# Four fixed PSUM places and a new order of jobs in an attention kernel with experts behind it

## The chip, the cores and the metric

The program runs on one core of one Trainium2 chip. The metric is the device time of one execution in microseconds (us), and less is better. The engines are named as the profile names them: PE (TensorE, with its weight loads as PEld), DVE (VectorE), ACT (ScalarE), POOL (GpSimd) and SP (SyncE, which here only issues DMAs). They run side by side and wait for each other on semaphores. PSUM, where matmuls write, has eight banks of 512 floats in each of 128 partitions.

## The reference

The first half is attention for 8 batches of 8 heads, 576 positions and 64 columns a head. The second is a layer of 8 experts, of which each token goes through one.

```
q_rot, k_rot = rotate(q), rotate(k)
scores = scale * q_rot @ k_rot^T;  scores -= max(scores)
attn = exp(scores);  attn /= sum(attn) + 1e-9
x = attn @ v, as [4608 tokens, 512]
logits = x @ w_gate + modality_bias[modality_id];  e = argmax(logits)
gate = softmax(logits)[e]
out = gate * (relu(x @ w1[e]) @ w2[e])
```

## The kernel before

Two heads make a pair, and there are 32 pairs (NPAIR), four to a batch. For each pair n the kernel does these jobs, whose names are used below:

- LD and LD1 load q and k of the pair, transposed, from DRAM (two halves), and LV loads v.
- T1, T2, R, HI, LO make the rotated q and k: two products, a sum, a rounded high part HL[:, 0] (HI, on ACT) and the rest HL[:, 1] (LO). T1, T2, R and LO run on POOL except at the start. The tiles HL and SW exist twice, for even and odd pairs.
- SWH and SWL are DMAs by SP that put the two heads' halves of HL's high and low part into SW with partitions exchanged.
- S0 to S8 are score blocks of 128 queries on PE: 64-row matmuls on HL and SW, six for S0 to S7 and twelve for S8, which takes the last 64 queries of both heads. Each fills both banks of a double place `[128, 2, 512]` in PSUM. MNu is the row minimum on DVE (the scores carry a minus sign, so it is the maximum), and EXu the exponential on ACT, which also adds up the row into `sum`.
- F0 to F3, FA and FB ("fills") are PE transposes of the exponentials, 82 in all, again into a double place. A_F is the copy of its first bank to SBUF by ACT, and B_F that of its second by DVE.
- AVA and AVB multiply by v on PE (queries 0 to 255 and 256 to 575), OTA and OTB copy the result on ACT, and OUT transposes it back on PE together with the gate's weights.
- re and ri: the sums plus 1e-9 on ACT (line 406), and their reciprocal on DVE (line 409). EVA and EVB are `ev` on DVE (lines 434 to 438), which multiplies OUT's two banks by ri into X, G and XT.
- After the fourth pair of a batch, XO writes the batch's X to DRAM (SP, one DMA of 1 MB and two small ones), BIAS and the steps RK of `route` find each token's expert (POOL, DVE, ACT, one set of small PE matmuls at RK8), and the scatters SC write rows of a table (POOL).

Each job has a key, its place in one long list: the key in KEYS plus 14.438 times the pair's number (PER). The list is sorted by key and its jobs are emitted one after the other. PE, ACT, DVE, POOL and SP each keep the order of emission, so the keys alone set what stands behind what on each engine; they are not times that anything waits for. The first two and the last two pairs have keys of their own in AT (`first`, `second`, `last2`, `last`), as have the batch work and the first expert's jobs.

PSUM is divided in two. RING has three double places that scores and fills take in turn; the pool psA has two single banks for AV, OUT and the rank matmuls of RK8. A matmul that takes a place waits until its last reader has ended; `free` removes the wait for the minimum, since the exponential has waited for it already.

After the attention come blocks of 256 tokens that go through one expert each: m_l1 and m_l2 are the two matmuls, with weights split into a high and a low part on ACT and DVE (m_hi, m_lo), gathered rows transposed on DVE (m_tr) and split (m_tre). The first block's L1 is emitted among the last pair's jobs, into places of the ring.

Of the kernel before, what the change touches and what calls it, by code (L numbers as in the profile page):

```python
# [8 lines left out]
F32 = mybir.dt.float32  # L9
# [9 lines left out]
P = 128  # L19
# [22 lines left out]
    "FB": 8.21, "A_FB": 8.89, "B_FB": 9.00, "AVA": 11.22, "OTA": 13.98, "AVB": 14.84, "OTB": 18.19, "OUT": 19.01,  # L42
    "EVA": 25.51, "EVB": 20.38, "RE": 11.27, "RI": 15.89, "XO": 27.00, "T1": -32.78, "T2": -26.38,
    "R": -23.03, "LO": -15.27, "HI": -18.83, "SWH": -17.41, "SWL": -11.79, "LD": -39.33, "LV": -10.14,
}
AT = dict(
    rk=(23.0, 28.55, 31.2, 36.9, 41.45, 43.0, 44.4, 45.7, 54.6, 56.9, 57.4, 58.85, 60.2, 70.35, 73.3),
    bias=15.6,
    sc=(73.4, 87.85, 102.3, 116.7, 116.75),
    sce=(73.4, 73.45, 87.85, 87.9, 102.3),  # L50
    pl=(58.9, 70.4, 73.35, 84.85, 87.75, 99.3, 102.2, 113.7, 116.6),
    plan=(-49.7, -35.2, 6.0, 9.0),
    ix=(-41.5, -3.9, 6.1, 9.1),
    sine=-48.9,
    rows=(((0, -27.5, None), (1, -13.05, None), (2, -12.4, None), (3, -2.9, (30, "av", 0)), (5, 0.45, (30, "av", 1)),
           (7, 4.75, (30, "out", 1))), ((0, 11.15, ("l1", 0)),), ((0, 16.5, None),)),
    w1=(-21.6, -21.5, -16.2, -16.1),
    w2=(-9.9, -9.8, -9.7, -9.6),
    hi=(-14.8, -14.7, -0.4, -0.3),
    lo=(-11.8, -1.6, 10.8, 10.85),  # L60
    tr=(10.2, 10.21),
    te=(10.3, 10.4),
    hi2=(10.5, 10.98, 11.1, 11.2),
    lo2=(11.5, 11.55, 11.65, 11.75),
    last=dict(F2=7.0, A_F2=7.75, B_F2=7.75, FB=7.5, A_FB=8.3, B_FB=8.3, FA=8.35, A_FA=8.8, B_FA=8.8, AVB=10.3, AVA=10.4, RE=10.2,
              RI=10.25, OTB=10.96, OTA=11.0, OUT=11.21, EVB=11.35, EVA=11.4, XO=11.9),
    last2=dict(EVA=24.55),
    l1=(11.1, 11.3, 11.4, 11.42),
    l1e=(11.3, 11.6, 11.7, 11.8),
    w1n=(11.85, 11.86, 11.87, 11.88),  # L70
    end=12.0,

    first=dict(S1=-5.9, S0=-5.86, MN1=-5.82, MN0=-5.74, EX1=-5.7, EX0=-5.66, S6=-5.58, S7=-5.54, MN6=-5.5,
        EX6=-5.42, MN7=-5.34, EX7=-5.3, S3=-5.26, S2=-5.22, MN3=-5.18, EX3=-5.14, F0=-5.1, MN2=-5.06,
        A_F0=-5.02, B_F0=-4.98, EX2=-4.94, F3=-4.9, S4=-4.86, A_F3=-4.82, B_F3=-4.78, MN4=-4.74, S5=-4.7,
        EX4=-4.66, MN5=-4.62, EX5=-4.58, S8=-4.54, MN8=-4.5, EX8=-4.46, LV=-2.9),
    second=dict(T1=-20.22, T2=-20.06, R=-19.9, HI=-19.82),
    consts=(44.4, 51.3),
    setdma=(-2.85, 8.0, 22.5, 30.1),
    sine3=-47.5,  # L80
)
PIN = "PE,Activation,DVE,Pool"
# [3 lines left out]
def tile_attention_moe(ctx: ExitStack, tc: tile.TileContext, qk, v, mod, wg, mb, w1, w2, rope, cf, ci, out):  # L86
# [45 lines left out]
    psA = att.enter_context(tc.tile_pool(name="psA", bufs=2, space=PSUM))  # L132
# [26 lines left out]
    RING = [psS.tile([P, 2, 512], F32, name=f"ps{i}") for i in range(3)]  # L159
    lastmin = [None] * 3  # L160
    turn = [0]

    def ring():
        i = turn[0] % 3
        turn[0] += 1
        seen, lastmin[i] = lastmin[i], None
        return i, RING[i], seen

# [134 lines left out]
    def scores(n, u):  # L303
        d = st[n]
        ri, ps, seen = ring()
        d["ring", u] = ri
# [3 lines left out]
        for m, (hh, wq, wk) in enumerate(L):  # L310
            for g in range(2):
                t = d["HL" if g == hh else "SW"][g * 64:g * 64 + 64]
                k0 = K1 if g else K0
                free(nc.tensor.matmul(ps[:, g, 0:288], t[:, wq, q0:q0 + P], t[:, wk, k0:k0 + 288],  # L314
                                      start=(m == 0), stop=(m == len(L) - 1)), seen)
# [4 lines left out]
    def rowmin(n, u):  # L320
        d = st[n]
        mn = sm.tile([P, 1], F32, name="mn", tag="mn", bufs=6)
        lastmin[d["ring", u]] = nc.vector.tensor_reduce(mn, d["S", u][:, :, 0:288], op=ALU.min, axis=AX.XY).ins  # L323
        d["m", u] = mn

    def expo(n, u):
# [4 lines left out]
                             bias=d.pop(("m", u)), scale=-1.0, accum_out=d["sum"][:, u:u + 1])  # L331


    def tpose(ps, g, c, src, k0):
        r = slice(g * 64, g * 64 + 64)
        free(nc.tensor.transpose(ps[0][:, g, c:c + 64], src[r, k0:k0 + P], idf[r, r]), ps[1])  # L336

    def fill(n, f):
        d = st[n]
        ps = ring()[1:]  # L340
        d[f] = ps[0]
# [19 lines left out]
    def evac(n, f, g):  # L361
        d = st[n]
        ps = d[f][:, g]
        mine, other = (d.setdefault((f, x), []) for x in (g, 1 - g))

# [19 lines left out]
    def AV(n, half):  # L385
        d = st[n]
        c0, c1 = (0, 256) if half == 0 else (256, 576)
        pa = d["pa", half] = psA.tile([P, 512], F32, name="pa", tag="pa")
        for kt in range(5):
            for hh in range(2):  # L390
                r = PH[:, 4 * hh + kt, c0:c1] if kt < 4 else PD[:, c0:c1]
                i = nc.tensor.matmul(pa[hh * 64:hh * 64 + 64, 0:c1 - c0], d["V"][:, hh, kt, :], r, start=(kt == 0), stop=(kt == 4))  # L392
                d.setdefault(("av", half), i.ins)

    def avout(n, half):
        d = st[n]
        c0, c1 = (0, 256) if half == 0 else (256, 576)
        acopy(OT[n % 2][:, c0:c1], d.pop(("pa", half))[:, 0:c1 - c0])

    bt_ = {}  # L400

    def rsum(n, part):
        d = st[n]
        if part == 0:
            d["re"] = sm.tile([P, 9], F32, name="re", tag="re")
            nc.scalar.activation(d["re"], d["sum"], AF.Identity, bias=EPS)
        else:
            d["ri"] = sm.tile([P, 9], F32, name="ri", tag="ri")
            nc.vector.reciprocal(d["ri"], d["re"])

    def outp(n):
# [5 lines left out]
        po = [psA.tile([P, 512], F32, name="pa", tag="pa") for _ in range(2)]  # L417
        for i in range(5):
            for h in range(2):
                c = (i * P, 448 if h and i == 4 else i * P)[h]  # L420
                r = slice(h * 64, h * 64 + 64)
                x = nc.tensor.matmul(po[h][:, i * 72:i * 72 + 72], oT[r, c:c + P], RW[r, hp, :], start=True, stop=True)
                d.setdefault(("out", h), x.ins)
        d["po"] = po

    def ev(n, h):
# [11 lines left out]
        nc.vector.tensor_scalar(Bt["xt"][r, :, hp, :], po[r, 288:360].rearrange("p (o c) -> p o c", o=2), ri[r, 8:9], None, op0=ALU.mult)  # L438

# [12 lines left out]
    def route(b):  # L452
# [46 lines left out]
        pm = bank("H") if b == B - 1 else psA.tile([P, 512], F32, name="pa", tag="pa")  # L499
        pr = pm[:, 0:48].rearrange("p (j e) -> p j e", e=E)  # L500
        nc.tensor.matmul(pr, UT, OH, start=True, stop=False)
        for j in range(5):
            nc.tensor.matmul(pr[:, j + 1:6, :], ON, OH[:, j:j + 1, :].to_broadcast([P, 5 - j, E]), start=False, stop=(j == 4))
# [3 lines left out]
        V_.tensor_tensor(RUN[:, b + 1, :], pr[:, 5, :], RUN[:, b, :], op=ALU.add)  # L507
        yield
# [230 lines left out]
    spare = []  # L739
# [466 lines left out]
```

## Time and profile before

| | us |
|---|---|
| three timed runs | 933.55, 936.58, 946.05 |
| their median | 936.58 |
| the profiled execution | 934.42 |
| its span, first to last instruction | 932.6 |
| PE busy in the span | 894.4 (96%) |
| DVE, ACT, POOL busy | 682.6, 623.0, 659.1 |

The attention stage takes about the first 490 us, and the experts the rest. The profile's rows carry start and duration in us, the engine, the line of the kernel, and output<-inputs by tile names with buffer numbers left out: `ps` is any place of RING, `pa` a bank of psA, `P` the exponentials, `PH` and `PD` the transposed ones, `ST` the loaded q and k or weights, `mn` a row minimum. A PE row's end is modelled, so starts are more to be trusted than durations. In a row of a stretch of the span the columns are the stretch, its length, then busy us and instructions of PE, PEld, DVE, ACT and POOL, the granted clock, the share of the DMA engines, and GB/s.

### The profile page before, as it was taken

To read this page: it belongs to the slowest core of one execution; us is meant where nothing else is said; L and a number is where in the kernel's file an instruction comes from. 1 tells how busy PE (TensorE), PEld (TensorE's weight loads), DVE (VectorE), ACT (ScalarE), POOL (GpSimd) and SP (SyncE) were. 2 spreads that over 40 slices of the span, in tenths; PEclk is the share of its full clock that TensorE was granted. 3 is DMA by queue.
4 is the path that set the end of the run, shared out by engine and by line. 5 is a ranking of instruction groups with operands and counts; after the bars stand their busy time and mean duration, and the time that the engine had idled before them with its cause. 6 is when DMAs were issued, how large, how long until landed. Compare 5 with 4: busy or idle time off the path is not lost.

```text
span 932.6 us, 24974 instructions
## 1 busy us (share of the span) xinstructions
PE 894.4 (96%) x9248; PEld 738.7 (79%) x9248; DVE 682.6 (73%) x1221; ACT 623.0 (67%) x1291; POOL 659.1 (71%) x494
## 2 busy tenths in 40 slices
PE   2999999999999999999999999999999999999996
PEld 2777777777777777777677888888888899789996
DVE  7678788877878778787886878766666666666663
ACT  3778787787877878778783655565555555455652
POOL 4988879889888988999833677566576665556410
PEclk9999999999999999999999999999999999999999
DMA  8865757678586885856752631127635112511240
GB/s 265 246 178 171 238 157 201 196 175 238 156 199 190 184 229 155 200 179 180 203 163 75 154 109 35 55 75 244 202 97 189 50 57 92 170 57 37 79 154 21
DMA packets 82301, 141.10 MB, mean 151 GB/s; under 512 B 28635, under 2 KB 52589, under 8 KB 81148
## 3 DMA queue, kind: packets, MB, share of 16 engines
q1 hardware_dynamic: 71660, 118.25, 44.9%
q0 software_dynamic: 9248, 19.46, 6.8%
q10 hardware_dynamic: 1264, 1.72, 0.6%
q8 instruction: 75, 1.23, 0.6%
q14 instruction: 54, 0.44, 0.2%
HBM read 140.33 MB, written 19.51 MB: 171 GB/s over the span
## 4 chain that ended last, share of the span: by engine, by line
PE 67%; ACT 16%; DVE 9%; issue 4%; another core or an unknown queue 1%; DMA 1%; POOL 0%; DVEq 0%; POOLq 0%; ACTq 0%
PE psH L860 22%; PE psY L883 21%; ACT P L330 13%; PE ps L314 10%; PE pa L392 9%; DVE mn L323 6%; PE ps L336 5%; ACT PH L274 2%; DMA SW<-HL 1%; DVE PH L368 1%; DMA ST<-in_qk_dram 1%; ACT HL L274 0%; ACT W2H L274 0%; DVE PD L368 0%
## 5 line engine op out<-in xcount | busy, mean ns | idle before, releaser
L330 ACT ACTIVATE P<-ps,mn 128x576 f32<-128x576 f32 x288 | 210.4, 737 | 94.1 <-DVE mn L323 94.1
L323 DVE TENSOR_REDUCE mn<-ps 128x1 f32<-128x576 f32 x288 | 204.1, 745 | 82.9 <-PE ps L314 37.3
L795 POOL DMA_INDIRECT XG<-X,iy x148 | 181.7, 1228 | 66.8 <-issue 50.2
L860 PE MATMUL psH<-HL,W1H 128*128 128x256 f32 x1152 | 202.6, 279 | 0.0
L314 PE MATMUL ps<-SW 64*128 64x288 f32 x960 | 166.4, 313 | 15.2 <-DMA SW<-HL 15.2
L860 PEld LDWEIGHTS psH<-HL,W1H 128*128 128x128 f32 x1152 | 176.8, 188 | 1.6
L314 PE MATMUL ps<-HL 64*128 64x288 f32 x960 | 165.9, 312 | 1.6 <-ACT P L330 1.5
L860 PE MATMUL psH<-HL,W1L 128*128 128x256 f32 x576 | 160.8, 279 | 0.2 <-DVE W1L L271 0.2
L314 PEld LDWEIGHTS ps<-HL 64*128 64x128 f32 x960 | 136.5, 189 | 23.5 <-issue 12.1
L314 PEld LDWEIGHTS ps<-SW 64*128 64x128 f32 x960 | 134.3, 189 | 26.2 <-DMA SW<-HL 13.5
L271 DVE TENSOR_TENSOR W1L<-ST,W1H 128x1024 fp32r<-128x1024 f32 x76 | 90.3, 1223 | 76.6 <-ACT W1H L274 68.8
L392 PE MATMUL pa<-PH,V 128*64 128x320 f32 (+1 forms) x1024 | 138.2, 412 | 0.0
L888 POOL DMA_INDIRECT out_dram<-y,ix x36 | 46.2, 1284 | 115.3 <-ACT y L886 69.7
L883 PE MATMUL psY<-W2H,SW 128*128 128x512 f32 (+1 forms) x304 | 118.8, 391 | 1.9 <-issue 1.5
L883 PE MATMUL psY<-W2L,SW 128*128 128x512 f32 (+1 forms) x304 | 119.7, 394 | 0.0
L336 PE MATMUL ps<-idf,P 64*128 64x64 f32 x2624 | 110.6, 229 | 9.5 <-ACT P L330 3.4
L336 PEld LDWEIGHTS ps<-idf,P 64*128 64x128 f32 x2624 | 93.2, 140 | 25.4 <-ACT PH L274 9.0
L291 POOL TENSOR_TENSOR HL<-ST,HL 128x1216 fp32r<-128x1216 f32 x31 | 85.9, 2772 | 33.1 <-ACT HL L274 33.1
L860 PEld LDWEIGHTS psH<-HL,W1L 128*128 128x128 f32 x576 | 108.3, 188 | 0.4 <-DVE W1L L271 0.4
L392 PEld LDWEIGHTS pa<-PH,V 128*64 128x64 f32 x1024 | 67.9, 136 | 48.4 <-issue 10.0
L368 DVE COPY PH<-ps 128x512 f32<-128x512 f32 (+1 forms) x160 | 96.0, 629 | 10.2 <-PE ps L336 9.3
L271 DVE TENSOR_TENSOR W2L<-ST,W2H 128x1024 fp32r<-128x1024 f32 x76 | 92.5, 1218 | 4.2 <-ACT W2H L274 3.6
(197 smaller groups left out, 1575.7 us busy)
## 6 DMA issues: line engine op xcount, KB each, us to landing
ST<-in_moe_w_dram SPq DMA_DIRECT2D x152, 512.0 KB
ST<-in_qk_dram SPq DMA_DIRECT2D x62, 608.0 KB
SW<-HL SPq DMA_DIRECT2D x124, 232.0 KB
V<-in_v_dram SPq DMA_DIRECT2D x32, 256.0 KB
X<-X SPq DMA_DIRECT2D x8, 1024.0 KB
XG<-X,iy POOLq DMA_INDIRECT x148
V<-in_v_dram SPq DMA_DIRECT2D x64, 16.0 KB
X<-XT SPq DMA_DIRECT2D x16, 64.0 KB
```

The costliest lines, as they stand in the source:

```text
L271: nc.vector.tensor_tensor(o, a, b, op=ALU.subtract)
L291: e.tensor_tensor(d["HL"][:, 1, c], a, d["HL"][:, 0, c].bitcast(F32), op=ALU.subtract)
L314: free(nc.tensor.matmul(ps[:, g, 0:288], t[:, wq, q0:q0 + P], t[:, wk, k0:k0 + 288], start=(m == 0), stop=(m == len(L) - 1)), seen)
L323: lastmin[d["ring", u]] = nc.vector.tensor_reduce(mn, d["S", u][:, :, 0:288], op=ALU.min, axis=AX.XY).ins
L330: nc.scalar.activation(p.rearrange("p (a b) -> p a b", a=2), ps[:, :, 0:288], AF.Exp, bias=d.pop(("m", u)), scale=-1.0, accum_out=d["sum"] ...
L336: free(nc.tensor.transpose(ps[0][:, g, c:c + 64], src[r, k0:k0 + P], idf[r, r]), ps[1])
L368: mine.append((nc.vector.tensor_copy if g else acopy)(o, i).ins)
L392: i = nc.tensor.matmul(pa[hh * 64:hh * 64 + 64, 0:c1 - c0], d["V"][:, hh, kt, :], r, start=(kt == 0), stop=(kt == 4))
L795: inst = nc.gpsimd.indirect_dma_start(out=XG[s % 2][:, t, g, :], out_offset=None, in_=X.rearrange("n (i f) -> (n i) f", f=P)[0:rows], in_o ...
L860: l1_[s] = nc.tensor.matmul(ps[:, i, :], w[:, c, f0:f0 + P], x[:, c, :], start=(m == 0), stop=(m == 11)).ins
L883: nc.tensor.matmul(ps, hx[:, c, t * P:(t + 1) * P], x[:, c, h * w:h * w + w], start=(m == 0), stop=(m == 23))
L888: inst = nc.gpsimd.indirect_dma_start(out=out.rearrange("n (i f) -> (n i) f", f=w) if nh > 1 else out, out_offset=bass.IndirectOffsetOnAxi ...
```

## The change

There are four parts.

1. PSUM becomes one set of four double places SL. Scores, fills and OUT take both banks of a place, AVA and AVB one bank, and RK8 one bank. A table SLOTS says which place each job takes; if it isn't idle in the order of emission, another that has been idle longest is taken. A bank counts as idle once the job that reads it last has been emitted (`give`). RING and psA go.
2. KEYS is replaced, and with it the order of all jobs of a pair on PE, ACT, DVE, POOL and SP. The batch work (BIAS, RK0 to RK14, SC0 to SC4) and LD1 are in the same table now, the first expert's jobs in a table MOE, and AFTER holds what the gathers wait for.
3. The first two pairs keep an order of their own for some jobs (EDGE); the last two pairs follow KEYS.
4. The sum's guard and the reciprocal become one job RI on DVE.

```
 KEYS = {
+    "S0": 4.14, "MN0": 4.15, "EX0": 6.38, "S1": -0.75, "MN1": 0.49, "EX1": 0.96, "S2": -3.41, "MN2": -1.89, "EX2": 0.16, "S3": -6.54,
+    "MN3": -3.18, "EX3": -1.90, "S4": -7.65, "MN4": -6.15, "EX4": -4.71, "S5": -9.23, "MN5": -8.96, "EX5": -7.24, "S6": -11.86, "MN6":
+    -10.68, "EX6": -8.87, "S7": -4.99, "MN7": -2.67, "EX7": -0.77, "S8": -14.04, "MN8": -12.86, "EX8": -12.07, "F0": 7.62, "A_F0": 8.97,
+    "B_F0": 9.28, "F1": 7.75, "A_F1": 10.33, "B_F1": 9.87, "F2": -0.67, "A_F2": 0.90, "B_F2": 0.90, "F3": 1.74, "A_F3": 2.36, "B_F3":
+    1.96, "FA": 6.38, "A_FA": 7.35, "B_FA": 7.28, "FB": 1.85, "A_FB": 4.00, "B_FB": 2.71, "AVA": 11.22, "AVB": 6.10, "OTA": 15.05,
+    "OTB": 7.76, "OUT": 16.47, "EVB": 21.70, "EVA": 18.17, "RI": 9.89, "T1": -34.83, "T2": -32.09, "R": -28.61, "LO": -19.61, "HI":
+    -23.39, "SWH": -18.86, "SWL": -18.48, "LD": -40.45, "LD1": -51.82, "LV": 4.14, "XO": 23.88, "BIAS": 24.03, "RK0": 24.74, "RK1":
...
 }
+SLOTS = {
+    "S0": 3, "S1": 2, "S2": 3, "S3": 2, "S4": 3, "S5": 0, "S6": 1, "S7": 0, "S8": 3, "F0": 0, "F1": 1, "F2": 0, "F3": 1, "FA": 1, "FB":
+    0, "AVA": 1, "AVB": 2, "OUT": 2, "RK8": 5, "L1": 0,
+}
...
+MOE = dict(
...
+    l1=(12.000, 18.000, 22.400, 22.500),
...
+    end=25.0,
+)
...
-    RING = [psS.tile([P, 2, 512], F32, name=f"ps{i}") for i in range(3)]
+    SL = [psS.tile([P, 2, 512], F32, name=f"ps{i}") for i in range(4)]
+    idle = {(i, b): i * 2 + b for i in range(4) for b in range(2)}
+    def take(nm, bks):
+        own = SLOTS[nm]
...
+        if not all((own, b) in idle for b in bks):
...
+                own = min((i for i in range(4) if all((i, b) in idle for b in bks)), key=lambda i: max(idle[i, b] for b in bks))
...
+    def give(own, *bks):
+        for b in bks:
+            idle[own, b] = clock[0]
+            clock[0] += 1
...
-            nc.scalar.activation(d["re"], d["sum"], AF.Identity, bias=EPS)
+        nc.vector.tensor_scalar(d["re"], d["sum"], 1e-9, None, op0=ALU.add)
+        d["ri"] = sm.tile([P, 9], F32, name="ri", tag="ri")
+        nc.vector.reciprocal(d["ri"], d["re"])
```

In the old table XO had 27.00, SWH -17.41, SWL -11.79, EVA 25.51, EVB 20.38, LO -15.27, LV -10.14 and S8 -5.22. A job of pair n+3 has 43.314 added when it is compared with one of pair n.

More of the change, by code (lines that the diff above doesn't have):

```diff
@@ L387, in AV @@
         c0, c1 = (0, 256) if half == 0 else (256, 576)
-        pa = d["pa", half] = psA.tile([P, 512], F32, name="pa", tag="pa")
+        own, _, seen = take("AV" + "AB"[half], (half,))
+        pa = d["pa", half] = SL[own][:, half, :]
+        d["at", "av", half] = own
         for kt in range(5):
@@ L416, in outp @@
             bt_[b] = dict(x=xo.tile([P, 4, DM], F32, name="X", tag="X"), xt=xo.tile([P, 2, 4, 36], F32, name="XT", tag="XT", bufs=2))
-        po = [psA.tile([P, 512], F32, name="pa", tag="pa") for _ in range(2)]
+        own, _, seen = take("OUT", (0, 1))
+        po = [SL[own][:, h, :] for h in range(2)]
+        d["at", "out"] = own
         for i in range(5):
@@ L507, in route @@
         V_.tensor_tensor(RUN[:, b + 1, :], pr[:, 5, :], RUN[:, b, :], op=ALU.add)
+        if b < B - 1:
+            give(own, bk)
         yield
@@ L948, in tile_attention_moe @@
         K_("OUT", outp, n)
-        for w in range(2):
-            K_("R" + "EI"[w], rsum, n, w)
+        K_("RI", rsum, n)
         if n > 0:
@@ L991, in tile_attention_moe @@
[L991 to L998 removed]
+            for i, x in enumerate(steps):
+                K_(f"RK{i}", *x)
@@ L999, in tile_attention_moe @@
+    for i in range(2):
+        J(MOE["consts"][i], "consts", 0, setup2, i)
+        Z("place", i, weights2, i)
+        Z("tr", i, m_tr, 0, i)
+        Z("te", i, m_tre, 0, i)
+    g = plan0()
+    for i in range(9):
+        Z("pl", i, next, g, None)
     for s in range(3):
         for i in range(8):
-            k_, after = [x for x in A["rows"][s] if x[0] <= i][-1][1:]
-            Z(k_ + 0.01 * i, m_gather, s, i // 4, i % 4, after)
-    for i in range(2):
-        Z(min((A["hi2"], A["lo2"])[i]) - 0.01, weights2, i)
@@ L1005, in tile_attention_moe @@
[L1005 to L1018 removed]
+            Z("rows", 8 * s + i, m_gather, s, i // 4, i % 4, AFTER.get((s, i)))
```

204 lines of the change are left out of this document (89 added, 115 removed), and 13 rows, old and new, of tables (EDGE, KEYS).

## The prediction

> **What bounds the kernel now.** I read the page's busy shares first, then the stretches of the span, then the chain that ended last, and then one pair's rows in the timeline.
>
> ```profile
> span 932.6 us, 24974 instructions
> PE 894.4 (96%) x9248; PEld 738.7 (79%) x9248; DVE 682.6 (73%) x1221; ACT 623.0 (67%) x1291; POOL 659.1 (71%) x494
> ...
> PE 67%; ACT 16%; DVE 9%; issue 4%; another core or an unknown queue 1%; DMA 1%; POOL 0%; DVEq 0%; POOLq 0%; ACTq 0%
> ...
> 100.00:475.00 375.00, 368.67 (x5210) 280.16 (x5206) 299.69 (x669) 299.44 (x787) 323.19 (x219) 1.00 0.72 193
> ...
> 63.51 2.31 PE pa L392 x20
> 213.59 2.84 PE pa L392 x20
> 444.86 2.31 PE pa L392 x20
> ```
>
> TensorE looks full, 96%, but the ends of matmuls are modelled, and a quarter of the chain lies on ACT and DVE. So there is waiting inside "busy". The change touches the attention stage (to about 490 us) and the hand-over to the experts, and the two 2.31 rows give its pace: AVA of pair 2 starts at 63.51, AVA of pair 28 at 444.86, so a pair takes 381.35 / 26 = **14.67 us**. What TensorE needs for a pair comes from the timeline:
>
> ```profile
> 227.24 0.29 PE L314 MATMUL ps<-HL 64*128 64x288 f32 x1
> 227.50 0.29 PE L314 MATMUL ps<-HL 64*128 64x288 f32 x1
> ...
> 231.73 2.09 DVE L323 TENSOR_REDUCE mn<-ps 128x1 f32<-128x576 f32 x3 [1.56 <-ACT P L330]
> ...
> 232.25 1.24 PE L422 MATMUL pa<-RW,oT 64*128 64x72 f32 x20
> 232.53 0.74 ACT L330 ACTIVATE P<-ps,mn 128x576 f32<-128x576 f32 x1 [0.49 <-DVE mn L323]
> ...
> 233.41 1.78 PE L336 MATMUL ps<-idf,P 64*128 64x64 f32 x36
> ...
> 233.97 0.74 ACT L330 ACTIVATE P<-ps,mn 128x576 f32<-128x576 f32 x1
> ...
> 234.36 1.28 DVE L368 COPY PH<-ps 128x512 f32<-128x512 f32 x2
> ...
> 234.69 1.09 ACT L274 ACTIVATE PH<-ps 128x512 f32<-128x512 f32 x2
> ...
> 235.34 1.65 PE L336 MATMUL ps<-idf,P 64*128 64x64 f32 x46
> ...
> 236.94 0.37 PE L314 MATMUL ps<-HL 64*128 64x288 f32 x1
> 237.59 1.23 ACT L274 ACTIVATE HL<-ST 128x1216 fp32r<-128x1216 f32 x1
> ...
> 238.90 2.77 POOL L291 TENSOR_TENSOR HL<-ST,HL 128x1216 fp32r<-128x1216 f32 x1 [1.33 <-ACT HL L274]
> ```
>
> Two HL matmuls 0.26 apart with an SW matmul beside each are 0.13 a step, 0.065 a score matmul: 60 of them, 3.9 us. The 46 transposes take 1.65 with the last one's end, about 0.03 each: 82 are 2.5 us, but from 233.41 to 236.94 they took 3.53. OUT runs from 232.25 to 233.41, 1.16, of which some 0.1 waits. AVA and AVB are 2.31 + 2.84. The sum without waits is 3.9 + 2.5 + 1.07 + 5.15 = 12.6, and 2.0 us of each pair is waits and switches. The largest piece is the clump of six fills, a good 1.0: three double places rotate, and each fill waits for copies of 0.5 to 0.7.
>
> **Prices of the other engines.** Row minima back to back are 0.67 apart (three in 2.09), exponentials 0.72 (232.53 to 233.97 is two), copies of a fill 0.60 to 0.68 on DVE and 0.48 to 0.60 on ACT, HI 1.23, each rope step on POOL 2.77.
>
> **The change, part by part.** *Places.* RING's three and the two pa banks become four double places; nothing is added on an engine. *Guard.* The ACT step re leaves, and one small tensor_scalar comes to DVE ahead of the reciprocal:
>
> ```profile
> L406 ACT ACTIVATE re<-sum,EPS x32: 293/304/307, 34.0 to 490.2; 128x9 f32<-128x9 f32 x32
> ...
> L481 DVE TENSOR_SCALAR vv<-dl 128x40 f32<-128x40 f32 x1 | 0.2, 185 | 0.0
> ```
>
> 0.3 off ACT, about 0.2 onto DVE, per pair. It stands before the row minimum of S3', where DVE is the later engine; were there no slack, its cost would be 0.2 x 31 = 6 us, and it can gain at most 0.3 x 31 = 9. I take it as part of the walk below. *Order.* On TensorE a pair now runs (one prime is the next pair, two the one after, n the pair whose fills run): F0, F1, S3', S7', S2', AVA, S1', F2', S8'', F3', FB', OUT, S6'', S0', S5'', AVB', FA', S4''. Scores stand between the fills, so copies run beside them.
>
> I walk this order with the prices above, from F0 = 0. S4' of the round before needs a row minimum (0.28 to 0.95), then come the copies of F0 and F1 on DVE (to 1.63 and 2.23). S3' runs 0.96 to 1.47 in place 2; S7' needs place 0 back from F0's copies, 1.69; S2' follows to 2.68; AVA needs place 1 back from F1 and runs 2.68 to 4.99. S1' to 5.49, F2' to 5.97, S8'' to 6.85, F3' 7.33, FB' 7.76, OUT 8.82, S6'' 9.33, S0' 9.73, S5'' 10.22. AVB' wants place 2's bank from ev of OUT, which DVE ends at 10.2 after the copies of F2', F3' and FB': 10.26 to 13.10. FA' 13.23, S4'' 13.73, and F0' starts. So **13.73 a pair**, with 0.3 of waits left. POOL's batch work and the rank matmuls in every fourth pair (0.13 + 0.11) add some 0.1: 13.84. Gain 14.67 - 13.84 = 0.83, over the 29 pairs between S8(2) and S8(31): **-24.0 us**.
>
> Switches are in the walk at row prices: the first step of scores after transposes takes 0.21 instead of 0.13 (281.11 to 281.32 below), and I take 0.1 at each entry to AV and each exit from it too; five blocks of scores a pair against three. No row shows S followed by a fill. Below, it is nothing, as S4 to OUT costs nothing in the rows; above, 0.11 a switch, 0.33 a pair, 10 us in all. I take nothing, OUT being the nearest case, and keep the 10 for the range.
>
> The Trainium skill, "TensorEngine Tiling (Array Packing)", Key Properties, says that changing the tiling mode drains the engine while another tile of the same mode does not. Scores, fills and OUT are 64*128 and only AV is 128*64, with two entries each before and after, so by the page none of the added switches costs; the sum would be some 5 us lower. The 0.21 step after transposes of the same mode, quoted below, speaks against the page here.
>
> *What is moved on SP.* XO, the write of a batch's X after every fourth pair n, stood after SWH(n+3); now it stands ahead of both SWH(n+3) and SWL(n+3) (23.88 against 24.45 and 24.83), and SP works in order. Before:
>
> ```profile
> 268.27 1.13 SPq L299 DMA_DIRECT2D SW<-HL  x2
> 269.49 0.54 SPq L443 DMA_DIRECT2D X<-X  x1
> 270.08 2.54 SPq L445 DMA_DIRECT2D X<-XT  x2
> 272.71 2.20 SPq L299 DMA_DIRECT2D SW<-HL  x2
> ...
> 268.82 0.30 DVE L438 TENSOR_SCALAR XT<-pa,ri 64x72 f32<-64x72 f32 x1
> ...
> 281.11 0.38 PE L314 MATMUL ps<-HL 64*128 64x288 f32 x1
> ...
> 281.32 0.29 PE L314 MATMUL ps<-HL 64*128 64x288 f32 x1
> ...
> 269.50:279.40 9.90, 9.68 (x128) 6.86 (x122) 7.70 (x16) 7.49 (x21) 9.47 (x8) 1.00 0.96 237
> ...
> 8.47 1.18 SPq L299 DMA_DIRECT2D SW<-HL  x2
> ...
> 12.88 0.61 PE L314 MATMUL ps<-SW 64*128 64x288 f32 x1 [12.88 <-DMA SW<-HL]
> ```
>
> The last ev ends at 269.12, X is issued at 269.49, the low swap at 272.71, and S8(18) starts at 281.11 unhindered: 11.6 us from X to S8. In the walk the last ev (EVB, behind MN5'') ends at 13.05, X goes at 13.4, and S8(n+3) is due at 5.97 + 13.73 = 19.70: **6.3 us**, with two swaps behind X instead of one. What they need: at the least 3.2 of issue for X and XT, 2.3 for four swap issues, and 3.2 from the last issue to the release (9.65 to 12.88), 8.7 in all, so S8 waits 2.4. At the most, the 11.6 were all needed and a second 2.2 comes on top: 7.5. By bytes, X 1024 KB, XT 128 and the swaps 928, 2.08 MB at the 237 GB/s of that stretch, 8.8 plus about 1.1 to start: 9.9, so 3.6. I take 3.6; nothing hides it, as TensorE works in order and S8 heads the round. Seven batches (n = 3 to 27): **+25.2 us**, from 16.8 to 52; beyond 5 a batch I hold little, since then nothing would have been spare before.
>
> *The other moves.* LV stands after the swaps, some 9 us before AVB needs it; LD and LD1 a pair ahead. POOL runs T1 between R and LO as before. *Ends.* Pair 31 loses its own order. By the walk, OT of half A stands behind four casts of W2 and the first expert's L1E, so OUT(31) waits 1.35, and L1 starts 2.0 after AVA where it now starts its second matmul late by 0.46:
>
> ```profile
> 494.10 0.60 PE L392 MATMUL pa<-PD,V 128*64 128x256 f32 x4
> ...
> 495.49 0.39 PE L860 MATMUL ps<-HL,W1H 128*128 128x256 f32 x1 [0.46 <-DVE HL L271]
> ...
> 496.48 2.00 ACT L274 ACTIVATE W2H<-ST 128x1024 fp32r<-128x1024 f32 x2
> ...
> 511.98 0.49 PE L883 MATMUL psY<-W2H,SW 128*128 128x512 f32 x1 [0.43 <-ACT SW L869]
> ```
>
> With 1.0 for fills that have no next pair's scores between them, that is 1.35 + 1.55 + 1.0 = 3.9 more, and about 1.3 comes back in the first L2, whose waits (0.43 and smaller ones) fall away: **+2.6**, between 0 and 6. The first pair I hold even. The other 18 blocks are not touched.
>
> Sum, against the profiled execution's own 934.4 (span 932.6 and 1.8 around it): 934.4 - 24.0 + 25.2 + 2.6 = **938**. The median of the runs shown, 936.6, is 2 above that execution.
>
> **The rivals.** *The order's gain without the wait at X* (the swaps land in time, or ev stands earlier): for it, the DMA engines have idle time and the swaps are small; against it, SP's own issue time of 5.5 nearly fills the 6.3. With at most 1 us a batch: 938 - 25.2 + 1 = 914. *POOL becomes the ring that sets the pace*, the slower case. POOL worked 323.19 in 375 us, 12.64 a pair; if LO goes on to wait for HI, 1.33 as in the row, with 0.3 of issue gaps, that is 14.3 a pair, and the low swap is late for S8 in every pair: HI cannot start before S0', the last reader of that HL, ends near 10, so LO ends near 14.0 and the swap lands near 18.3 for an S8 at 19.70. It decides once POOL is 1.4 late. Price (14.3 - 13.84) x 29 = 13, and 1 us more in each batch's pair with two table writes: 958. *Switches at their upper price*: 948. *The order does nothing*, because the copies are as late as now: the 14.67 stays and X still waits: 962; S between the fills speaks against it.
>
> **How the numbers follow.** Forecast 0.52, its own range 925 to 952 (2.4 to 5 a batch, and 0.25 a pair either way); the first rival 0.24, 910 to 920; POOL 0.10; switches 0.10; no effect of the order 0.04. The range that leaves out no more than 2 in 10 is 912 to 955. Against 936.6, and 2% (18.7, what a measurement tells from no change) either way, 918 and 955: faster 0.22, slower 0.14, within 0.64.
>
> **What would show it.** Right: AVA to AVA 13.7 to 13.9 in pairs without X, no waits between fills, and seven waits of S8 for the swap DMA of 2.4 to 5 us. Wrong: the swap's landing without a wait (then 914), LO's wait for HI grown and S8 waiting in most pairs (958), or fills that still pause for copies.

## The result, and the profile after

The changed kernel takes **1015.2 us** (median of four runs, 1009.4 to 1016.2) against 936.7 before: **1.081 times as long, 95% interval 1.072 to 1.090**. The forecast was 938, the range 912 to 955. The profiled execution has a span of 1014.4 us, 81.8 more than before.

From the page of the changed kernel (busy times) and from the stretch that was quoted for before:

```profile
span 1014.4 us, 24926 instructions
PE 924.0 (91%) x9248; PEld 762.7 (75%) x9248; DVE 726.9 (72%) x1253; ACT 624.1 (62%) x1259; POOL 660.0 (65%) x494
...
100.00:475.00 375.00, 342.55 (x4528) 261.92 (x4525) 294.09 (x602) 260.04 (x662) 284.31 (x184) 0.93 0.61 168
```

The work is the same (9248 matmuls), but in the same 375 us only 4528 of them start instead of 5210, and the granted clock is 0.93 where it was 1.00. If the clock is always either whole or half, as the 0.50 in the rows further down suggests, 0.07 / 0.5 x 375, some 52 us, ran at half clock; this is an estimate.

To find where the 81.8 went, I cut both spans at the last AV block of pairs 0, 30 and 31. First the rows of after (line L421), with pairs 2, 6, 7 and 28 too, then the three of before (L392):

```profile
47.45 0.44 PE L421 MATMUL ps<-PH,V 128*64 128x256 f32 x2
75.93 0.65 PE L421 MATMUL ps<-PH,V 128*64 128x256 f32 x3
166.53 0.65 PE L421 MATMUL ps<-PH,V 128*64 128x256 f32 x3
188.68 0.44 PE L421 MATMUL ps<-PH,V 128*64 128x256 f32 x2
507.97 0.44 PE L421 MATMUL ps<-PH,V 128*64 128x256 f32 x2
546.36 0.44 PE L421 MATMUL ps<-PH,V 128*64 128x256 f32 x2
564.97 0.44 PE L421 MATMUL ps<-PH,V 128*64 128x256 f32 x2 [3.42 <-ACT PH L297]
```

```profile
37.97 0.76 PE L392 MATMUL pa<-PH,V 128*64 128x320 f32 x4
480.20 0.49 PE L392 MATMUL pa<-PH,V 128*64 128x320 f32 x2
492.38 0.82 PE L392 MATMUL pa<-PH,V 128*64 128x256 f32 x6
```

Front 47.45 against 37.97, **+9.5**; 30 pairs 498.9 against 442.2, **+56.7**; last pair 18.6 against 12.2, +6.4; the rest to the end 449.4 against 440.2, +9.2. (For pairs 0 and 30 the last AV block is AVB in before and AVA in after, so the front of after holds a little more work, about 1 us by the rows.) Between pair 2 and pair 28 a pair took 16.6 us, where 13.84 was predicted without X and 14.7 with it. The pairs are not alike. Eleven of the 30, among them the one ahead of each X, take 14.2 to 14.6. The one that holds a batch's X takes 18.4 to 22.2 (22.1 from 166.53 to 188.68), the one behind it 15.0 to 19.0, and the next mostly 15 to 16. The pair of 22.1, from the timeline of SP, VectorE and TensorE, and the stretches behind it:

```profile
163.66 0.27 DVE L470 TENSOR_SCALAR XT<-ps,ri 64x72 f32<-64x72 f32 x1
163.68 0.33 SPq L476 DMA_DIRECT2D X<-X  x1
164.10 2.12 SPq L478 DMA_DIRECT2D X<-XT  x2
166.31 3.30 SPq L322 DMA_DIRECT2D SW<-HL  x4
...
170.48 0.40 PE L338 MATMUL ps<-HL 64*128 64x288 f32 x1
172.24 0.39 PE L338 MATMUL ps<-SW 64*128 64x288 f32 x1 [1.36 <-DMA SW<-HL]
174.18 0.60 PE L338 MATMUL ps<-SW 64*128 64x288 f32 x1 [1.54 <-DMA SW<-HL]
...
177.13 2.15 PE L453 MATMUL ps<-RW,oT 64*128 64x72 f32 x18
...
171.00:175.00 4.00, 1.22 (x8) 1.01 (x10) 0.67 (x2) 0.94 (x3) 1.78 (x1) 0.74 1.02 309
175.00:179.00 4.00, 4.00 (x56) 4.00 (x54) 2.39 (x5) 1.85 (x6) 0.00 (x0) 0.50 0.33 129
179.00:183.00 4.00, 4.00 (x29) 3.13 (x29) 2.96 (x6) 2.13 (x4) 0.83 (x1) 0.50 0.00 0
183.00:187.00 4.00, 4.00 (x61) 2.63 (x59) 1.63 (x6) 2.29 (x7) 3.65 (x5) 0.98 0.75 178
```

As predicted, X goes at the last ev, the swaps stand behind it, and S8, due at 170.48, gets its data in two waits; from 170.48 to F3 at 175.31 it takes 4.8 us instead of 0.9: 3.9 late, for 3.6 forecast, though its last steps already run at the lower clock. What the forecast did not have comes after: the clock column falls to 0.50 and stays there to 183, with TensorE busy all the time. OUT takes 2.15, where the walk had 1.06.

And the guard. Its group in after, and one of its 32 places, on VectorE and POOL:

```profile
L436 DVE TENSOR_SCALAR re<-sum x32: 152/1308/2624, 47.1 to 562.3; 128x9 f32<-128x9 f32 x32
...
164.43 2.78 POOL L306 TENSOR_TENSOR ST<-ST,ST 128x1216 f32<-128x1216 f32 x1
165.92 1.32 DVE L436 TENSOR_SCALAR re<-sum 128x9 f32<-128x9 f32 x1
167.27 0.21 DVE L438 RECIPROCAL ri<-re 128x9 f32<-128x9 f32 x1
167.29 2.78 POOL L310 TENSOR_TENSOR ST<-ST 128x1216 f32<-128x1216 f32 x1
```

Minimum, median and maximum of re are 152, 1308 and 2624 ns. It starts beside a rope step on POOL and ends when that step ends (164.43 + 2.78 = 167.21; 165.92 + 1.32 = 167.24). In 29 of the 32 places it ends 0.02 to 0.05 us after such a POOL step; the other three, at the end, have no long tensor step beside them and take 0.15 to 0.34. The reciprocal behind it runs beside the next rope step and takes 0.21.

### The profile page after: what moved, and what is told of

It is laid out like the page before. It is cut to its first block, busy times and chain, and to the rows that moved or that the text cites. A ratio compares the mean times of both kernels' runs of the same rounds, so it can differ in the third digit from the quotient of the medians.

```text
span 1014.4 us, 24926 instructions
## 1 busy us (share of the span) xinstructions
PE 924.0 (91%) x9248; PEld 762.7 (75%) x9248; DVE 726.9 (72%) x1253; ACT 624.1 (62%) x1259; POOL 660.0 (65%) x494
## 3 DMA queue, kind: packets, MB, share of 16 engines
q0 software_dynamic: 9248, 19.46, 6.2%
## 4 chain that ended last, share of the span: by engine, by line
PE 73%; DVE 9%; ACT 5%; DMA 5%; issue 3%; SPq 2%; another core or an unknown queue 2%; POOL 0%; POOLq 0%; DVEq 0%; ACTq 0%
PE psY L920 20%; PE psH L897 20%; PE ps L421 11%; PE ps L338 11%; PE ps L361 7%; DMA SW<-HL 4%; PE ps L453 4%; ACT P L354 3%; DVE re L436 2%; DVE PH L395 2%; DVE mn L347 2%; SPq L322 2%; ACT PH L297 1%; DMA ST<-in_qk_dram 1%
## 5 line engine op out<-in xcount | busy, mean ns | idle before, releaser
L338 PE MATMUL ps<-SW 64*128 64x288 f32 x960 | 190.5, 330 | 47.5 <-DMA SW<-HL 33.7
L833 POOL DMA_INDIRECT XG<-X,iy x148 | 175.9, 1188 | 73.6 <-issue 54.7
L338 PE MATMUL ps<-HL 64*128 64x288 f32 x960 | 197.2, 331 | 7.6 <-ACT P L354 6.9
L338 PEld LDWEIGHTS ps<-SW 64*128 64x128 f32 x960 | 143.6, 201 | 70.0 <-DMA SW<-HL 36.9
L421 PE MATMUL ps<-PH,V 128*64 128x256 f32 (+1 forms) x1024 | 146.1, 429 | 11.7 <-DVE PH L395 6.3
L338 PEld LDWEIGHTS ps<-HL 64*128 64x128 f32 x960 | 146.4, 200 | 13.1 <-ACT P L354 9.2
L361 PEld LDWEIGHTS ps<-idf,P 64*128 64x128 f32 x2624 | 108.4, 147 | 26.3 <-ACT P L354 20.0
L297 ACT ACTIVATE PH<-ps 128x512 f32<-128x512 f32 (+1 forms) x160 | 89.4, 559 | 53.7 <-PE ps L361 41.4
L361 PE MATMUL ps<-idf,P 64*128 64x64 f32 x2624 | 118.2, 235 | 3.5 <-ACT oT L297 1.4
L421 PEld LDWEIGHTS ps<-PH,V 128*64 128x64 f32 x1024 | 72.2, 142 | 63.7 <-issue 12.1
```

Of the source, the lines that this page charges most:

```text
L297: return nc.scalar.activation(o, i, AF.Copy, scale=scale)
L833: inst = nc.gpsimd.indirect_dma_start(out=XG[s % 2][:, t, g, :], out_offset=None, in_=X.rearrange("n (i f) -> (n i) f", f=P)[0:rows], in_o ...
```

## The experiments

Theory after this reading: XO's place costs a wait, and the wait costs the clock; the guard costs what is left of POOL's operation; the rest is at the two ends. Rivals: the router's work on POOL and VectorE makes the batch pairs late whatever XO does; VectorE hides the guard. All kernels were cut like the two above; runs named together shared a chip and the runs of before. Times are best compared within such a group, since some chips show late releases (below, at x_guard) that others don't.

| kernel | ratio to before (95%) | to pair 0 | 30 pairs | last pair | rest |
|---|---|---|---|---|---|
| before | 1 | 38.0 | 442.2 | 12.2 | 440.2 |
| after | 1.081 (1.072-1.090) | 47.5 | 498.9 | 18.6 | 449.4 |
| x_last | 1.044 (1.041-1.048) | 45.8 | 458.3 | 16.8 | 444.3 |
| warm | 1.062 (1.058-1.066) | 44.7 | 479.0 | 16.8 | 442.7 |
| guard_tt | 1.074 (1.069-1.079) | 45.6 | 498.0 | 16.8 | 442.3 |
| rows_late | 1.069 (1.061-1.076) | 45.2 | 491.9 | 16.8 | 438.2 |
| after_again | 1.083 (1.075-1.091) | 47.9 | 492.5 | 20.3 | 453.7 |
| guard_act | 1.067 (1.058-1.075) | 45.4 | 477.2 | 22.6 | 452.7 |
| x_guard | 1.031 (1.024-1.039) | 45.4 | 443.6 | 23.1 | 448.0 |
| b_guard | 1.072 (1.064-1.080) | 38.2 | 509.6 | 12.4 | 437.5 |
| lv | 1.021 (1.017-1.026) | 46.7 | 434.9 | 21.2 | 451.7 |
| lv_sc | 1.014 (1.010-1.019) | 46.4 | 432.0 | 20.6 | 451.0 |
| all | 1.011 (1.006-1.016) | 46.9 | 427.7 | 19.0 | 457.2 |
| guard_tr | 1.058 (1.053-1.063) | 47.1 | 477.2 | 16.8 | 443.9 |
| all_tr | 1.003 (1.001-1.005) | 47.7 | 430.5 | 14.3 | 440.2 |
| best | 0.992 (0.990-0.995) | 45.5 | 425.1 | 14.3 | 437.0 |

**x_last, warm, guard_tt, rows_late** ran together. *x_last* is one key:

```diff
-    ... "XO": 23.88,
+    ... "XO": 24.86,
```

> One key: the write of a batch's X (XO) goes behind both swaps of pair n+3 on SP instead of ahead of them. Theory: in each of 7 batches S8 waits 3.9 us for the swaps queued behind X, and the matmuls behind that wait run at a granted clock of 0.50 for some 8 us, which costs 3.7 us more, and some 2 us are late after that; all of it hangs on X standing first. Then S8 has no wait for the swap DMA over 1 us in a batch, the clock stays at 1.00 between 100 and 475 us, and the time is 1015 - 7 x (8.5 to 10) = 945 to 956. First rival: the loss comes from the batch's router steps and table writes on POOL, which make LO late: then the waits stay and the time is 1005 to 1015. Second rival: X has one buffer, and X written later holds up the next pair's ev on VectorE: waits of ev for a DMA appear, and the time is 965 to 990.

970.6 us. The first theory's place is right, its size is not: the 30 pairs fall by 33.6 (458.3 against the 491.9 of rows_late, whose attention stage is that of after), 4.8 a batch, not 8.5 to 10. The first rival is out; the time lies in the second rival's range, but ev never waits for a DMA. The stretch from 100 to 475 us and one wait of TensorE:

```profile
100.00:475.00 375.00, 350.13 (x4960) 268.65 (x4959) 328.63 (x663) 283.13 (x724) 314.71 (x208) 0.99 0.68 182
...
PE ps L421 <- DMA V<-in_v_dram: 4.4, 4, 1.6
```

The clock is back at 0.99, and part of the gain is given back at once: now V's load stands behind X on SP, and AV waits for it.

*warm* keeps XO and lets TensorE work through the wait:

```diff
         heads = (0, 1) if u == 8 else (u % 2,)
+        if u == 8 and n > 4 and n % 4 == 2:
+            t = HL[1 - n % 2][:, 0, 0:288]
+            for _ in range(30):
+                for g in range(2):
+                    r = t[g * 64:g * 64 + 64]
+                    free(nc.tensor.matmul(ps[:, g, 0:288], r[:, 0:P], r, start=True, stop=True), seen[g])
```

> XO stays ahead of the swaps; in front of the six score steps of S8 of each batch's pair (n = 6, 10, ... 30), 60 matmuls of old data into the same place are added (30 steps of 0.13 us, 3.9 us in all), which the first real step overwrites. TensorE then works through the wait instead of standing. Theory (the clock is half of the loss): the rows behind S8 run at full clock, F3 0.5 instead of 0.95, OUT 1.1 instead of 2.04, AVB 2.3 to 2.9 instead of 3.55; 3 to 4 us a batch come back, 1015 - 7 x 3.7 = 989, between 984 and 996. Rival (what is late behind the wait is late because of the copies and row minima queued on the other engines, not the clock): 1008 to 1020.

986.7 us. The pair that took 22.1 in after, with the added matmuls (L337) and the first real step behind them, and the clock of the long stretch:

```profile
163.33 0.65 PE L427 MATMUL ps<-PH,V 128*64 128x256 f32 x3
167.18 4.22 PE L337 MATMUL ps<-HL 64*128 64x288 f32 x60
171.24 0.42 PE L344 MATMUL ps<-SW 64*128 64x288 f32 x2
181.71 0.44 PE L427 MATMUL ps<-PH,V 128*64 128x256 f32 x2
...
100.00:475.00 375.00, 358.68 (x5078) 281.12 (x5074) 305.35 (x632) 270.93 (x689) 300.33 (x197) 0.98 0.65 176
```

The pair takes 18.4 us in all seven batches, at a granted clock of 1.00, where rows_late has 18.7 to 22.7, 20.3 in the mean, and the pair ahead of it takes 14.4. The 4.0 that are left in warm are the added matmuls' own time; no score step behind them waits, so they show only that the wait is not longer. The wait itself is read from rows_late: from S8 to F3 it takes 2.6 to 4.6 us longer than the usual 0.90, **3.6** in the mean. Behind it, from F3 to FA, warm takes 6.23 in every batch, as pairs without X do, and rows_late **2.3** more in the mean. So the half clock is a cause of its own: more matmuls, less time.

The 30 pairs fall by 13 (491.9 - 479.0), half of the 26 that I expected. The 3.7 a batch was worked out as if all seven pairs were like the one of 22.1; in rows_late only two are like it (granted clock 0.77 over 22.3 and 22.7 us), one has 0.83 and four 0.91. The total lies in the expected range, but that range was counted from after's 1015, and rows_late, beside it, takes 995.8: that agreement is in part luck.

*guard_tt*:

```diff
-        nc.vector.tensor_scalar(d["re"], d["sum"], 1e-9, None, op0=ALU.add)
+        nc.vector.tensor_tensor(d["re"], d["sum"], EPS.to_broadcast([P, 9]), op=ALU.add)
```

> The guard's addition stays on VectorE at its place, as a tensor_tensor with a column of 1e-9 instead of a tensor_scalar with a constant. Theory (the tensor_scalar waits until the operation then running on POOL is over, its median 1.31 us against 0.15 when POOL stands): re takes 0.15 to 0.25 us in all 32 pairs, and the time falls by 0.2 to 0.7 us a pair, to 993 to 1009. Rival (the duration is a wait for the sums or for the tile, which any form pays): median re stays over 1 us and the time within 4 us of 1015.

```profile
L436 DVE TENSOR_TENSOR re<-sum,EPS x32: 152/1229/3308, 45.2 to 557.7; 128x9 f32<-128x9 f32 x32
```

This form waits as long, and the expectation fell. Whether every form does was left to guard_tr.

*rows_late* put the last eight keys of `rows` at 25.20 to 25.27, as the gathers of slot 2 stood before.

> The eight gathers of slot 2 go behind the first expert's second layer, as they stood before the change, instead of directly behind the eight of slot 1. Theory (POOL's sixteen gathers in a row hold up the first expert: the ScalarE step behind L1 starts at 595.35, 12 us after L1's last matmul row and 0.5 us after the last gather): the wait of that step falls from 17.0 to about 6 us, and the time by 8 to 12 us, to 1003 to 1007. Rival (the wait has another cause, the weights or TensorE's own end): the wait stays over 14 us and the time within 4 us of 1015.

995.8 us. The wait of 17 us was in none of these four profiles, so it can't be judged here; the part behind the last pair is 4 us shorter than in warm and guard_tt (438.2 against 442.7 and 442.3).

**after_again, guard_act, x_guard, b_guard** ran together.

> The changed kernel as it is, once more, so that the other kernels can be held against it on one chip, and to see whether the wait of 17.0 us on ScalarE behind the first expert's L1 comes again: it was 5 us or less in four other kernels with the same order there. Theory (a single event of that one execution): no wait over 6 us there, and the time 1.07 to 1.08 times the kernel before. Rival (it belongs to the kernel): 17 us again.

1013.8 us, and the theory fell: the wait is there again.

```profile
ACT SW L906 <- remote: 19.8, 1, 19.8
```

*guard_act*: the guard is again a step of its own on ScalarE.

```diff
-        nc.vector.tensor_scalar(d["re"], d["sum"], 1e-9, None, op0=ALU.add)
+        nc.scalar.activation(d["re"], d["sum"], AF.Identity, bias=EPS)      # a job of its own, RE
-    "RI": 9.89
+    "RE": 10.40, "RI": 13.00
```

> The changed kernel with the guard back on ScalarE (key 10.40, behind A_F1) and the reciprocal at 13.00 on VectorE. Theory (re on VectorE stands until POOL's running operation ends, and the row minima behind it are late by what it lasts, 1.3 us in the mean, of which the order hides some): the reciprocal stays at 0.2, nothing of that line is left on VectorE, and 0.3 to 0.7 us a pair come back: 9 to 22 us less than the changed kernel. Rival (the minima have that slack): within 4 us of the changed kernel.

998.5 us, 15.3 below after_again, and the 30 pairs are shorter by the same 15.3: 0.5 a pair. The pairs that neither X nor a batch's router work touches now take 13.82 to 14.0; the two behind X's mostly 15.4 and 14.1 to 14.5.

> Both at once: XO behind the swaps and the guard on ScalarE. Theory: with XO behind the swaps the two pairs of each batch that still took 16.4 and 16.6 us did so because re lasted 2.5 and 3.3 us beside POOL's rope and the exponentials behind it were 3 to 4 us late; without it these pairs take 14.2 to 14.6 too. 7 x 2 x 2.0 = 28 us and 0.2 in the other pairs, so the time is 30 us below XO alone: 1.005 to 1.02 times the kernel before. Rival (these pairs are late because of the router's steps and V's load behind X): less than 8 us below XO alone, 1.035 to 1.045.

964.8 us. The 30 pairs fall by 33.5 against guard_act, as in x_last, to 443.6; but 1.031 lies between theory and rival. In most batches two pairs still take 15.1 to 15.5 instead of 13.85. One is V's, as in x_last. The other is new (POOL, TensorE, ScalarE, VectorE):

```profile
303.39 0.95 POOL L574 DMA_INDIRECT TAB<-VAL,oi  x1 [0.17 <-issue]
304.65 0.99 POOL L574 DMA_INDIRECT TAB<-VAL,oi  x1 [0.31 <-issue]
...
303.22 0.92 PE L361 MATMUL ps<-idf,P 64*128 64x64 f32 x20
...
306.39 0.60 ACT L297 ACTIVATE PH<-ps 128x512 f32<-128x512 f32 x1 [1.46 <-PE ps L338]
306.40 0.69 DVE L395 COPY PH<-ps 128x512 f32<-128x512 f32 x1 [1.76 <-PE ps L338]
```

F1's transposes end at 304.14, its copies on two engines start at 306.4, though both engines are free from 304.93 at the latest. The profile names a score matmul as the releaser, which these copies do not read. I take it that TensorE's release reached them 2.2 us late, while POOL issued two table writes; that is inferred.

*b_guard* is the kernel before with `nc.vector.tensor_scalar(d["re"], d["sum"], 1e-9, None, op0=ALU.add)` in the place of ScalarE's step.

> The kernel before with one part of the change alone: the guard as a tensor_scalar on VectorE, at the key where ScalarE had it. Theory: re lasts 1.0 to 1.6 us in the mean beside POOL, as in the changed kernel, not the 0.15 to 0.2 of the small operations; TensorE's places come free later by part of it, and the time rises by 3 to 20 us (0.1 to 0.6 a pair). Rival (the duration belongs to the new order, or VectorE has the slack): re at 0.2, or the time within 2 us.

1001.9 us beside 934.0: **one instruction of nine columns costs 68 us**, 2.2 a pair, over three times the upper end of what was expected.

```profile
L406 DVE TENSOR_SCALAR re<-sum x32: 173/1996/2582, 34.1 to 559.1; 128x9 f32<-128x9 f32 x32
...
235.16 2.76 POOL L291 TENSOR_TENSOR HL<-ST,HL 128x1216 fp32r<-128x1216 f32 x1 [1.46 <-ACT HL L274]
235.96 1.99 DVE L406 TENSOR_SCALAR re<-sum 128x9 f32<-128x9 f32 x1
...
PE ps L314 <- ACT P L330: 41.9, 31, 2.0
```

In that order re comes in 29 of the 32 pairs just after POOL's LO has begun and lasts to its end (237.92 and 237.95); the minima behind it are 2 us late, then the exponentials, and TensorE waits for those up to 2.0 us, in 31 rows.

**lv, lv_sc, all** ran together, each on top of x_guard: `"LV": -4.60` for 4.14; then also `"SC0": 81.09, "SC1": 95.53, "SC2": 109.97, "SC3": 124.40, "SC4": 109.98`; then also `te=(10.450, 10.460)` and rows_late's keys.

> XO behind the swaps and the guard on ScalarE as in the run before, and one key more: V's load (LV) goes ahead of the swaps (-4.60 instead of 4.14). Theory: of the two slow pairs of a batch (15.5 and 15.6 us against 13.85) one is slow because V stands behind X on SP and lands 1.4 us late for AVB; then these pairs fall to 13.9 to 14.2, the waits of AV for V's DMA go, and the time is 7 x 1.4 = 10 us lower: 1.016 to 1.024 times the kernel before. Rival (VectorE's router steps make them slow): within 3 us of 1.031.

> As lv, and the five table writes of a batch on POOL go ahead of LO, into AVB's time, instead of ahead of T2 in AVA's. Theory: while POOL issues two table writes in a row, TensorE's releases reach the other engines 2.2 us late (F1's end in the row at 304.14, the copies of F1 on both engines at 306.4), and the other slow pair of a batch is slow by that; where the releases come late at all on this chip, the pairs after it fall from 15.4 to 14.0 to 14.5 and 7 to 10 us are gained against lv. Rival (the slow pair comes from the rank matmuls and the router's reductions): within 3 us of lv. On a chip where no release is late in the profile, within 2 us of lv too.

> As lv_sc, with the end mended as well: the first expert's tre steps go behind the copies of F1 (10.45 instead of 10.30 and 10.40), and the eight gathers of slot 2 behind the first expert's second layer, as before the change. Theory: AVA of pair 31 no longer waits 3.0 us for a copy that stands behind a gather on ScalarE, and the first expert's step behind L1 no longer waits for sixteen gathers: 3 + 5 to 9 us against lv_sc, which makes 0.995 to 1.010 times the kernel before. Rival (the end is bound by the weights' casts, and the front's 7 us stay): 0 to 3 us against lv_sc.

954.4, 949.5 and 946.3 us. lv did what was expected: V's pair fell from 15.2-15.5 to 13.9-14.0. lv_sc: most pairs behind the table writes fell from 14.7-14.8 to 13.8-14.4, and one of 20.8 near the end to 16.1, but a pair of 15.5 and one of 18.8 came in; 2.9 us are gained in the 30 pairs, 5 in all, between theory and rival. all: the wait of AVA(31) behind the gather's step on ScalarE went, from 3.0 to 0.9 us, but the rest behind it grew by 6 in its profile, and the total is within the error of lv_sc's, close to the rival's 0 to 3.

**guard_tr** and **all_tr** ran together. In guard_tr the nine sums stand beside a column of 1e-9:

```diff
+    SUM = [cst.tile([P, 9, 2], F32, name=f"sum{i}") for i in range(3)]     # set to 1e-9 once
-        nc.vector.tensor_scalar(d["re"], d["sum"], 1e-9, None, op0=ALU.add)
+        nc.vector.tensor_reduce(d["re"], d["sum"], op=ALU.add, axis=AX.X)
```

(Not shown: the exponentials add up into column 0 of these tiles.)

> The changed kernel with the guard at its place on VectorE in a third form: the sums stand beside a column of 1e-9, and a tensor_reduce with one input adds the two. Theory (what waits for POOL is the form: tensor_scalar in its fast mode and tensor_tensor with two inputs from SBUF; a reduction with one input, like the reciprocal behind it, does not): re takes 0.15 to 0.25 us in all pairs, pairs without X fall from 14.2-14.5 to 13.8-13.9 as with the guard on ScalarE, and the time is 10 to 18 us below the changed kernel, 1.062 to 1.073 times the kernel before. Rival (the place is what counts, any step there waits): median re over 1 us and 1.075 to 1.09.

985.0 us, 1.058, a little below the expected range. Same engine, same place, another form:

```profile
L438 DVE TENSOR_REDUCE re<-sum x32: 152/154/164, 46.4 to 538.3; 128x9 f32<-128x18 f32 x32
```

It never lasts longer than 164 ns, and a pair that X and the router work leave alone takes 13.85. So the form waits, not the place. The Trainium skill, "SBUF — State Buffer", Who interferes with whom, states it so: VectorE and GpSimd share one pair of SBUF ports as an exclusive lock; a tensor_scalar in its two-port mode and a tensor_tensor with two inputs from SBUF take it, a tensor_reduce does not, and ScalarE never waits. All four agree with the medians here (1308, 1229, 154 ns, and ScalarE's steady 309); that the nine-column step runs in the two-port mode is inferred from its waiting.

> The run with everything mended (XO behind the swaps, V ahead of them, the table writes ahead of LO, the end's two keys), with this form of the guard instead of the one on ScalarE. Theory: ScalarE is 0.3 a pair lighter and the copies of the last pair stand behind nothing more; 0.997 to 1.010 times the kernel before, at most 6 us below the run with the guard on ScalarE. Rival (re waits as before): 1.02 or more.

933.6 us, 1.003 (1.001 to 1.005), inside the expected range: about the time of the kernel before. Against all it is 13 us less where 6 at most were expected, but all ran on a chip with late releases, so this is no measure of the guard. One pair of 21.8 us is left in it. LO stood behind two table writes in a row, ended at 412.77, and S8 waited 3.1 for the low swap:

```profile
409.04 0.91 POOL L573 DMA_INDIRECT TAB<-VAL,oi  x1 [0.30 <-issue]
409.96 2.81 POOL L317 TENSOR_TENSOR HL<-ST,HL 128x1216 fp32r<-128x1216 f32 x1
...
419.14 0.60 PE L341 MATMUL ps<-SW 64*128 64x288 f32 x1 [3.08 <-DMA SW<-HL]
```

*best* is all_tr with `"SC4": 75.93` and `lo2=(13.050, 13.060, 20.050, 22.650)`.

> As the run before, with two more moves: of the two table writes that stood in a row ahead of LO, one goes directly behind the router's last step (SC4 75.93), and the casts of the second weights' low halves on VectorE go behind the first expert's step that TensorE's L1 waits for. Theory: the one pair of 21.8 us (LO 1.9 us late behind two table writes, S8 waits 3.1 for the swap and runs on at half clock) becomes 14 to 15, and L1 no longer waits 2.2 us: 7 + 3 us less, 0.990 to 0.996 times the kernel before, the first that is faster than it. Rival (another wait takes the place, or the late pair was an event of one execution): 1.000 to 1.005.

**923.7 us, 0.992 times the kernel before (0.990 to 0.995)**: as expected, and the only version faster than both. It is less than the 2% that the prediction took for the least clear change, but the interval leaves out 1. Pairs 2 and 28, and the long stretch:

```profile
73.22 0.44 PE L423 MATMUL ps<-PH,V 128*64 128x256 f32 x2
440.08 0.44 PE L423 MATMUL ps<-PH,V 128*64 128x256 f32 x2
...
100.00:475.00 375.00, 366.50 (x5348) 285.74 (x5348) 313.69 (x718) 311.76 (x785) 327.85 (x222) 1.00 0.71 199
```

366.86 / 26 is 14.11 a pair, 0.56 less than before; 5348 matmuls start in the stretch, against 5210. One pair still takes 17.5 us in place of the 21.8.

## Why the prediction was wrong, step by step

*The walk of the new order* was right: 13.73 a pair forecast, 13.82 to 13.86 measured where neither the guard nor X, the router's work or a late release interferes (the first pairs of guard_act, most pairs of guard_tr and best). It is right block by block: AVA to F2', S8'' to F3', F3' to AVB' and AVB' to FA' take 2.81, 0.88, 3.41 and 2.84 in the walk, and 2.82, 0.89, 3.38 and 2.84 in pair 2 of guard_act. Against the 14.74 of before (442.2 / 30) that is the gain the sum counted on. The added switches from scores to fills cost nothing that the rows show: in after F3 starts 0.13 behind S8's last step, one step's time. That takes out the 948 rival. The Trainium skill, "TensorEngine Tiling (Array Packing)", Key Properties, has it so for tiles of one mode; the first score step behind fills still takes 0.21, as the walk had it. The 962 rival goes too, and POOL did not become the ring: in best it works 328 us of the 375, and the pairs still take 13.85.

*The guard* is the first step that failed, a term priced from the wrong row: 0.2, "at most 6 us", from one 185 ns tensor_scalar of the last batch. At that moment (522.0 of before) POOL was issuing a table write and had no long step of its own running. Beside POOL's rope steps it measured 1.3 in the median and cost 15 us in this order. The bound should have come from the step's neighbours on POOL, which was busy for 323 of 375 us. The Trainium skill, "SBUF — State Buffer", Who interferes with whom, states the rule, and the prediction did not weigh it.

*X ahead of the swaps* is the second: the wait was sized well, the price of the wait was not. 3.6 a batch was forecast (its "1.1 to start" is shown by no row of its own), and S8 to F3 takes 2.4 to 4.1 longer in after, 3.3 in the mean, and 3.6 in rows_late. But TensorE's clock falls behind it: F3 to FA takes 2.8 longer in after, 2.3 in rows_late and nothing in warm. Moving the one key back gains 33.6 (x_last) and 33.5 (x_guard) where 25.2 had been forecast; held against their neighbours, the seven pairs with X lose 6.5 each in after (20.9 in the mean); part of the difference is V's load, which stands behind X once X is moved. The reason I gave for holding little beyond 5, that nothing would have been spare before, speaks of the wait alone.

*"POOL's batch work adds 0.1"* held only where nothing else goes wrong: in best most batches have one pair of 14.1 and three of 13.85 or little more. In x_guard one pair of a batch was 1.5 late beside two table writes, and once X stood behind the swaps, V behind it was 1.4 late in another; no term of the sum had either.

*The ends*: +2.6 forecast, 0 for the front; +25.1 measured in after. The front cost 9.5: the first pair's F0 and F3 lost their early places between its scores, and TensorE stands where they stood (the row at 24.59), and then S8(1), now ahead of AV(0), waits for pair 1's low swap. TensorE also keeps half its pace longer: AVB of pair 0 takes 4.20, that of pair 1 2.37, and score steps are 0.24 apart until 39 us and 0.13 from 44, in before from 32 (the clock column reads 1.00 here, against these rows). In guard_tt, where AVB of pair 0 takes 2.38, the front is 45.6.

```profile
24.59 0.60 PE L338 MATMUL ps<-HL 64*128 64x288 f32 x1 [3.44 <-ACT P L354]
...
34.04 0.60 PE L338 MATMUL ps<-SW 64*128 64x288 f32 x1 [2.10 <-DMA SW<-HL]
...
39.46 4.20 PE L421 MATMUL ps<-PH,V 128*64 128x320 f32 x16
```

The last pair, without an order of its own, has no work beside its chain of fills and copies; it took 6.4 more, 4.6 in the four profiles of x_last's chip, and with the guard, te and the table writes mended 2.1. Behind it 9.2 more: in after and five other profiles the first expert's step comes 11 to 15 us after the last row of the L1 that it waits for; in the seven profiles without any wait labelled "remote" the rest takes 437 to 444, against 440.2.

```profile
583.09 0.28 PE L897 MATMUL ps<-HL,W1L 128*128 128x256 f32 x1
595.35 0.60 ACT L906 ACTIVATE SW<-ps 128x512 fp32r<-128x512 f32 x1 [16.99 <-remote]
```

Together, in the 30 pairs: the order -26.6 (0.89 a pair), X +45 (7 x 6.5), the guard +15, leaves some 23 of the +56.7. They lie in the two pairs behind each X: against 14.4 the first of them lose 17 in all and the second 6. What each of them waits for I have not split; table writes, rank steps and the guard beside them all fall there.

## What to carry to other kernels

Price a small VectorE step by what runs on POOL at that moment: beside long POOL operations, use a one-input reduction or ScalarE for it, since a nine-column tensor_scalar can cost two microseconds a round. Count a wait of TensorE together with the clock that it loses, and look at the clock column of the stretch behind it. When a write is moved ahead in an ordered queue, list everything behind it and move that too: the same order, with these places mended, went from 8% slower to 0.8% faster, each against the kernel before on its own chip. best was not run on a chip that shows late releases.

## What the runs showed of the hardware that was not expected

The clock fell without a long standstill: around waits of 1.36 and 1.54 us, with matmuls between them, it went down, and it was 0.50 for all of 175 to 183, though TensorE was busy through both stretches. The Trainium skill, "TensorE: Matmul & The Clock Gate", Part 1, gives about 3.4 us idle to lose the clock and about 3.4 busy to regain it; here less was enough to lose it. The time at half clock in the seven pairs with X of after, worked out from each pair's length and granted clock, is some 3.4 us in two, 7 in one and 10 in four (an estimate that takes the clock as whole or half), so it seems to come in lengths of about 3.4.

TensorE's releases seem to reach other engines late while POOL issues indirect DMAs: 2.2 us beside two table writes, 11 to 15 beside 15 or 16 gathers in a row. It goes with the chip, or with the time of the run, more than with the kernel. The late start of both copies comes four or five times in each of the profiles of after, after_again, guard_act and x_guard, and never in x_last, warm, guard_tt and rows_late, which have the same places for the table writes. Waits that the profile puts down to "remote", as at 595.35, stand in before, after and all seven profiles of the chips of after_again and lv, and in none of the seven of the other three chips. The kernel before takes 934 us on those two chips and 930 to 931 on the three. What holds the release back stays open.
